# Fused attention and MoE kernel on one core: larger w_in pieces, an even split of the first output products, loads one pair later

## The chip, the cores and the metric

The kernel runs on one core of a Trainium2 chip. The metric is device time in microseconds (us) of one execution, lower is better. Profile times are us from the start of the profiled execution's span. PE is the matrix engine, PEld its weight loads, DVE the vector engine, ACT the scalar engine, POOL the GpSimd engine, SP the engine whose queue issues most DMAs.

## The reference

Eight batches of 12 heads of attention (448 rows, head dimension 64) with a softmax that has one extra term in its denominator, then a two-layer feed-forward over the 3584 resulting rows:

```
scores = scale * q @ k^T ; m = max(scores) ; e = exp(scores - m)
attn   = e / (sum(e) + exp(-m) + 1e-9)
x      = (attn @ v), heads side by side          # 3584 x 768
h      = x @ w_in                                # 768 x 2048
g      = h * tanh(softplus(h))
out    = g @ w_out                               # 2048 x 768, float32
```

q, k, v, w_in and w_out come in as float32; the kernel casts them to bf16 and accumulates in float32.

## The kernel before, in words

**Units.** Two heads make a pair, six pairs a batch. Three pairs make a unit, so that a batch has two units and there are 16 units with attention (u = 0 to 15, counted from 0; the change's title counts them from one, and its units five and six are u = 4 and u = 5). The first two units, u = 0 and 1, are a head written out pair by pair (lines 552 to 577). From u = 2 on, the loop at line 579 does for each unit twelve steps, n = 0 to 11 (three pairs by four score tiles), and then eight blocks, f = 0 to 7, of the first feed-forward product of the batch before (`mm1_mish`). Each attention unit thus has an exponent phase, its twelve steps, and a feed-forward phase, its eight blocks. Two more units, u = 16 and 17, finish the feed-forward alone.

**One score step.** PE makes a tile of scores (L247, L250, L255 for the last tile of a pair), DVE takes its negated maximum (L269, `negm`), ACT the exponent (L282, `en`). DVE and POOL divide by the denominators (`normalise`, L317 on DVE, L315 on POOL). The transposed weights `eT` come back by a DMA transpose on SP's queue (L321) or, for five early pairs, by PE. `av_pair` (L354) multiplies them with v, and DVE casts the result into `xT` (L363).

**The output product** w_out (L443, `mm2_part`) of two batches is cut in parts: a tile of 128 rows by some quarters of 192 of the 768 columns. A part of nq quarters is eight chunks of two matmuls, each 192 times nq columns wide. `plan` says which parts fall in which unit. From u = 4 on the units are "grouped": `GROUPED`, and for u = 5 `GROUPED_LATE_AV`, list for each step n how many chunks PE does (`fill`), which score tiles it makes next (`sc`) and which pair's product with v it does (`av`). One PSUM bank, mo1, serves in turn each `av` and the last score tile of a pair, tiles 3, 7 and 11 of the unit (`last_sc`, L255). So L255 waits until DVE has cast that `av` into `xT`. Chunks use bank mo0. Finished parts are copied to `o_sb` by DVE (L430), at the next place that flushes, and stored by SP (L408).

**Loads.** `load_pair` puts three DMAs (q, k, v of a pair, 224 KB each) on SP's queue; `cast_pair` has POOL cast them (L171, L172, L158). In the unit loop both are called at n = 0, 3 and 6 (`LOAD_AT`): the load of the pair that lies `LEAD` = 4 ahead, and the cast of the one that lies 3 ahead. The pairs of the next unit are transposed on PE (L189) in the feed-forward phase at f = 1, 3, 5, and copied out by DVE (L208) and ACT (L218). Of each q a remainder is copied by POOL (L213, L214). SP's queue is in order: in a unit it has three DMA transposes, then loads and stores.

**Weights** are loaded by POOL's queue in pieces (`w_pieces`, `load_w`, L154), which cast to bf16 on the way: w_in in twelve pieces of 256 rows by 512 columns, and w_out in eight of 512 rows by 384 columns. `W_HEAD`, `W_AT` and line 668 say where. The first feed-forward phase (u = 2) reads columns 0 to 1023 of w_in, that of u = 3 the rest.

Of the kernel before, what the change touches and what calls it, by code (L numbers as in the profile page):

```python
# [15 lines left out]
UNIT_PAIRS = 3  # L16
# [3 lines left out]
def kernel(  # L20
# [12 lines left out]
    d_model, d_ff = moe_w_in.shape  # L33
# [8 lines left out]
    UNITS_PER_B = HP // UNIT_PAIRS  # L42
# [3 lines left out]
    NH = d_model // 2  # L46
# [85 lines left out]


    def w_pieces():
        c_in, c_out = d_ff // 4, NH
        for i in range(4):
            for a in range(0, DM_T, 2):
                yield (
                    w_in_sb[:, a : a + 2, i * c_in : (i + 1) * c_in],
                    moe_w_in[a * 128 : (a + 2) * 128, i * c_in : (i + 1) * c_in],  # L140
                )
        for h in range(2):
            for f in range(0, FF_T, 4):
                yield (
                    w_out_sb[:, f : f + 4, h * c_out : (h + 1) * c_out],
                    moe_w_out[f * 128 : (f + 4) * 128, h * c_out : (h + 1) * c_out],
                )
# [315 lines left out]
    plan = {}  # L463
    for g in range(B // 2):
        u0 = first_mm2 + 4 * g
        if g == 0:
            plan[u0] = [(0, 0, 0, 2), (0, 1, 0, 2), (0, 2, 0, 1)]
            plan[u0 + 1] = [(0, 0, 2, 2), (0, 1, 2, 2), (0, 2, 2, 2), (0, 2, 1, 1)]
        else:
            plan[u0] = plan.pop(u0) + [(g, 0, 0, 2), (g, 0, 2, 2), (g, 1, 0, 1)]  # L470
            plan[u0 + 1] = [(g, 1, 2, 2), (g, 2, 0, 2), (g, 2, 2, 2), (g, 1, 1, 1)]
        plan[u0 + 2] = [(g, 4, 0, 2), (g, 4, 2, 2), (g, 5, 0, 2), (g, 5, 2, 1)]
        plan[u0 + 3] = [(g, 3, 0, 2), (g, 3, 2, 2), (g, 6, 0, 2), (g, 5, 3, 1)]
        if g < B // 2 - 1:
            plan[u0 + 4] = [(g, 6, 2, 2)]
        else:
            plan[u0 + 3] += [(g, 6, 2, 1), (g, 6, 3, 1)]
# [5 lines left out]

    GROUPED = (
        [("fill", 8), ("av", 0)],
        [("fill", 2), ("sc", (3, 4, 5))],
        [("fill", 3)],
        [("fill", 3), ("sc", (6,)), ("av", 1)],
        [("fill", 3)],
        [("sc", (7, 8, 9))],  # L490
        [("fill", 3)],
        [("fill", 2), ("sc", (10,)), ("av", 2)],
        [("fill", 8)],
        [("sc", (11,))],
        [],
        [],
    )
# [2 lines left out]
        [("fill", 3), ("sc", (4, 5))],  # L500
        [("fill", 2)],
        [("fill", 3), ("sc", (6,)), ("av", 0)],
        [("fill", 3)],
        [("sc", (7, 8, 9))],
        [("fill", 3)],
        [("fill", 2), ("sc", (10,)), ("av", 1)],
        [("fill", 8)],
        [("sc", (11,))],
        [("av1", 2)],
        [],  # L510
# [19 lines left out]
        (5, 2): [(4, 0)], (5, 3): [(4, 1)],  # L530
    }
    AV_HEAD = {(3, 3): 0, (4, 2): 2, (4, 3): 1}
    W_HEAD = {0: 3, 1: 1, 3: 1, 4: 1}
    AV_AT = ({3: 4, 7: 3, 9: 5}, {5: 6, 8: 7, 10: 8})

    W_AT = ({5: 1, 9: 1}, {1: 1, 4: 1, 5: 1, 7: 1, 9: 1, 11: 1}, {3: 1, 5: 1, 7: 1, 9: 1})
    for which in ("qk", "v"):
        for p in range(UNIT_PAIRS):
            load_pair(p, which)
# [39 lines left out]
    for u in range(UNITS_PER_B, N_UNITS + 2 * UNITS_PER_B):  # L579
        attn = u < N_UNITS  # L580
        filler = deque()
        for part in plan.get(u, []):
            filler.extend(mm2_part(*part))
        total, done, acc = sum(w for _, w in filler), 0, 0.0
        p0 = u * UNIT_PAIRS
        grouped = attn and p0 >= GROUP_FROM
        if u == N_UNITS:
            mo_free.append(mo_tiles[1])
        end = min((u + 1) * UNIT_PAIRS, N_PAIRS) * STEPS

        for n in range(steps):
            pi, s = divmod(n, STEPS)
            p, idx = p0 + pi, p0 * STEPS + n
            late_tp = u == UNITS_PER_B and n == STEPS
            if late_tp:
                transpose_pair(p0 + 2)
            exps(idx)
            if grouped:
                flush_late()
                for what, arg in (GROUPED_LATE_AV if u == LATE_AV else GROUPED)[n]:  # L600
                    if what == "fill":
                        for _ in range(min(arg, len(filler))):
                            fn, w = filler.popleft()
                            fn()
                            done += w
                    elif what in ("av", "av1"):
                        bank = mo_tiles[1] if what == "av" else sc_tiles[1][:, 0, :]
                        av_pair(p0 - UNIT_PAIRS + arg, bank=bank)
                    else:
                        flush_late()  # L610
                        for i in arg:
                            scores(p0 * STEPS + i)
                if n in LOAD_AT:
                    load_pair(p0 + LOAD_AT.index(n) + LEAD)
                    cast_pair(p0 + LOAD_AT.index(n) + LEAD - 1)
                if u - UNITS_PER_B < len(W_AT):
                    load_w(W_AT[u - UNITS_PER_B].get(n, 0))
                continue
            if late_tp:
                evac_qk(p0 + 2)  # L620
            if u == UNITS_PER_B + 1:
                for part in TURN_AT[1].get(n, []):
                    turn_on_pe(*part)
            flush_late()
            acc += weight[n]
            want = int(total * acc / sum(weight) + 1e-6)
            while done < want:
                fn, w = filler.popleft()
                fn()
                done += w  # L630
            scores_ahead(end)
            if n in LOAD_AT:
                load_pair(p0 + LOAD_AT.index(n) + LEAD)
                cast_pair(p0 + LOAD_AT.index(n) + LEAD - 1)
            if u - UNITS_PER_B < len(AV_AT):
                early = AV_AT[u - UNITS_PER_B]
                if n in early:
                    av_pair(early[n])
                if u == UNITS_PER_B:
                    for part in TURN_AT[0].get(n, []):  # L640
                        turn_on_pe(*part)
            elif u == N_UNITS and n in LAST_AV_AT:
                av_pair(p0 - UNIT_PAIRS + LAST_AV_AT.index(n))
            if u - UNITS_PER_B < len(W_AT):
                load_w(W_AT[u - UNITS_PER_B].get(n, 0))
        assert done == total

        moe = u < N_UNITS + UNITS_PER_B
        b, w = (u - UNITS_PER_B) // UNITS_PER_B, u % UNITS_PER_B
        nxt = p0 + UNIT_PAIRS  # L650
        todo = sorted(range(p0, nxt), key=lambda p: p in BY_PE)
        to_group = attn and nxt >= GROUP_FROM
        if to_group and nxt == GROUP_FROM:
            flush_late()
            mo_free.remove(mo_tiles[1])
            rg["next"] = N_PAIRS * STEPS
        for f in range(FF_U):
            if f == FF_U - 1 and to_group and nxt < N_PAIRS:
                for s in range(3):
                    scores(nxt * STEPS + s)  # L660
            if moe:
                bank = sc_tiles[0][:, 0, :] if f == 1 else None
                if to_group:
                    bank = (sc_tiles[0][:, 0, :], None, mo_tiles[1])[MISH_BANK[f]]
                mm1_mish(b, w * FF_U + f, bank)
                if f == 2 and to_gather:
                    gather_mid(to_gather.popleft())
            if u == UNITS_PER_B and f in (2, 6):
                load_w(1)
            if not attn:  # L670
                continue
            if f == 0:
                denominators(att[p0]["whole"])
                normalise(todo[0], dma=todo[0] not in BY_PE)
            if f in (1, 3, 5):
                transpose_pair(nxt + f // 2, bank=f // 2 % 2)
                evac_qk(nxt + f // 2)
            if not to_group and f in (4, 6):
                scores_ahead(nxt * STEPS + f // 2 - 1)
            if f == FF_U - 1 and not to_group:  # L680
                scores_ahead(nxt * STEPS + 3)
            if f == 3:
                normalise(todo[1], dma=todo[1] not in BY_PE)
            if f == 4:
                normalise(todo[2], dma=todo[2] not in BY_PE, on_pool=True)
        if attn and u + 1 < N_UNITS:

            nc.scalar.activation(out=one, in_=zero, func=AF.Exp)
        if moe and w == UNITS_PER_B - 1:
            to_gather.append(b)  # L690
            if u == N_UNITS + UNITS_PER_B - 1:
                gather_mid(to_gather.popleft())
# [32 lines left out]
```

## Time and profile before

| | |
|---|---|
| time, median of 3 runs | 479.11 us (477.68 to 480.66) |
| the profiled execution's own time | 479.26 us |
| its span | 477.2 us, granted clock 0.986 on average |
| PE busy | 439.1 us, 92% |
| ACT, DVE, POOL busy | 346.6, 329.6, 193.5 us |
| mean share of the 16 DMA engines, hardware queues | 81.6% |
| mean share, POOL's software queue | 9.1%, 7488 packets |
| POOL's issue of one weight piece | 0.75 us |
| one unit in the steady part (u = 7 to 14) | 25.8 us |

PE's busy time counts matmuls from their start to a modelled end, so that a wait shorter than a matmul's own latency (0.33 us for 384 columns, against 0.16 us from one start to the next) is not shown as idle time. The table's shares are means over the whole run; the stretches differ. Up to about 100 us PE has long gaps and waits for ACT or DVE; from there on it is nearly always busy.

### The profile page before, as it was taken

How to read it: one execution, taken by the hardware profiler on the slowest of the kernel's cores; microseconds unless marked ns; L12 is line 12 of the kernel's file. 1: busy time of each engine (PE TensorE's matmuls, PEld its weight loads, DVE VectorE, ACT ScalarE, POOL GpSimd, SP SyncE). 2: the span in 40 equal slices, each digit the busy share in tenths (PEclk: the TensorE clock that was granted, in tenths of full speed). 3: DMA queues.
4: the chain of work that ended last, by engine and by line, in shares of the span. 5: the costliest groups of instructions: out<-in, count | busy, mean ns of one | idle time of the engine just before them, and what ended most of it. 6: DMA issues, size and time to landing. Idle time of an engine off the chain costs nothing.

```text
span 477.2 us, 8887 instructions
## 1 busy us (share of the span) xinstructions
PE 439.1 (92%) x3064; PEld 236.0 (49%) x3064; DVE 329.6 (69%) x652; ACT 346.6 (73%) x919; POOL 193.5 (41%) x365
## 2 busy tenths in 40 slices
PE   4565887898999899999999999999999999999997
PEld 2233544454445354545555454545454545555565
DVE  4888987968688687768686877778776868330021
ACT  5979778879796888979797969888897979412300
POOL 4877809364706345353635253434535340300000
PEclk9999698999999999999999999999999999999999
DMA  8999959999999999899998989998989594970213
GB/s 209 225 216 227 263 89 243 164 189 236 174 215 280 211 213 205 240 195 269 179 262 181 235 151 230 221 213 227 195 249 212 157 169 112 155 161 1 67 33 101
DMA packets 202381, 90.37 MB, mean 189 GB/s; under 512 B 159072, under 2 KB 198880, under 8 KB 202336
## 3 DMA queue, kind: packets, MB, share of 16 engines
q1 hardware_dynamic: 194848, 83.51, 81.6%
q0 software_dynamic: 7488, 6.29, 9.1%
q8 instruction: 24, 0.39, 0.3%
q14 instruction: 21, 0.17, 0.1%
HBM read 45.61 MB, written 11.01 MB: 119 GB/s over the span
## 4 chain that ended last, share of the span: by engine, by line
PE 70%; ACT 9%; DMA 8%; DVE 5%; POOL 3%; issue 2%; SPq 1%; DVEq 0%; ACTq 0%; POOLq 0%
PE mo L443 27%; PE mo L377 19%; ACT en L282 7%; PE mo L354 6%; PE sc L377 6%; PE sc L247 5%; DVE negm L269 3%; PE sc L189 3%; DMA w_out_sb<-in_moe_w_out_dram 2%; DMA v_f<-in_v_dram 2%; DMA eT<-en 2%; PE mo L255 2%; POOL en L315 1%; DMA w_in_sb<-in_moe_w_in_dram 1%; PE mo L189 1%
## 5 line engine op out<-in xcount | busy, mean ns | idle before, releaser
L282 ACT ACTIVATE en<-sc,negm 128x448 bf16<-128x448 f32 x300 | 186.2, 636 | 12.6 <-DVE negm L269 9.4
L269 DVE TENSOR_REDUCE negm<-sc 128x2 f32<-128x896 f32 (+1 forms) x156 | 158.3, 1047 | 26.1 <-PE sc L250 18.7
L443 PE MATMUL mo<-w_out_sb,gT 128*128 128x384 bf16 (+1 forms) x912 | 137.3, 301 | 1.0 <-DVE o_sb L430 0.5
L377 PE MATMUL mo<-xT,w_in_sb 128*128 128x448 bf16 x594 | 124.4, 352 | 0.6 <-DMA w_in_sb<-in_moe_w_in_dram 0.6
L443 PEld LDWEIGHTS <-gT 128*128 128x128 bf16 x912 | 80.9, 98 | 57.3 <-issue 21.3
L383 ACT ACTIVATE gT<-mo 128x448 bf16<-128x448 f32 x99 | 54.0, 547 | 73.1 <-PE mo L377 73.1
L377 PEld LDWEIGHTS <-w_in_sb 128*128 128x128 bf16 x768 | 71.7, 97 | 68.0 <-issue 8.9
L315 POOL TENSOR_SCALAR en<-en,rden 128x448 bf16<-128x448 bf16 x122 | 76.1, 641 | 55.7 <-DVE rden L307 52.8
L171 POOL CAST q_bf<-q_f 112x512 bf16<-112x512 f32 x47 | 28.9, 616 | 109.7 <-DMA q_f<-in_q_dram 109.0
L430 DVE COPY o_sb<-mo 128x192 f32<-128x192 f32 (+1 forms) x65 | 32.5, 499 | 56.6 <-PE mo L443 44.4
L282 ACT ACTIVATION_READ_ACCUMULATOR en<-sc,negm 128x1 f32 x300 | 62.2, 207 | 0.0
L317 DVE TENSOR_SCALAR en<-en,rden 128x448 bf16<-128x448 bf16 x214 | 60.5, 352 | 0.5
L247 PE MATMUL sc<-kT,qT 64*128 64x448 bf16 x144 | 47.1, 385 | 12.7 <-ACT en L282 11.2
L354 PE MATMUL mo<-eT,v_bf 112*64 112x448 bf16 x376 | 45.9, 367 | 3.0 <-DMA eT<-en 1.8
L250 PE MATMUL sc<-kT,qT 64*128 64x448 bf16 x144 | 47.4, 387 | 0.0
L377 PE MATMUL sc<-xT,w_in_sb 128*128 128x448 bf16 x174 | 37.6, 352 | 0.1
L363 DVE CAST xT<-mo 128x448 bf16<-128x448 f32 x44 | 27.0, 616 | 10.3 <-PE mo L354 9.6
L158 POOL CAST v_bf<-v_f 112x512 bf16<-112x512 f32 x48 | 29.5, 614 | 8.3 <-DMA v_f<-in_v_dram 8.0
L172 POOL CAST k_bf<-k_f 112x512 bf16<-112x512 f32 x47 | 28.8, 612 | 7.5 <-DMA k_f<-in_k_dram 7.3
L269 DVE TENSOR_REDUCE negm<-mo 128x1 f32<-128x448 f32 x36 | 22.3, 620 | 10.5 <-PE mo L255 10.5
L354 PEld LDWEIGHTS <-v_bf 112*64 112x64 bf16 x384 | 18.9, 111 | 21.6 <-issue 14.6
L282 ACT ACTIVATE en<-mo,negm 128x448 bf16<-128x448 f32 x36 | 23.1, 640 | 7.7 <-DVE negm L269 7.7
(55 smaller groups left out, 356.4 us busy)
## 6 DMA issues: line engine op xcount, KB each, us to landing
q_f<-in_q_dram SPq DMA_DIRECT2D x48, 224.0 KB, 5.0
k_f<-in_k_dram SPq DMA_DIRECT2D x48, 224.0 KB, 5.3
v_f<-in_v_dram SPq DMA_DIRECT2D x48, 224.0 KB, 5.5
w_in_sb<-in_moe_w_in_dram POOLq DMA_DIRECT2D x12, 256.0 KB, 5.9
w_out_sb<-in_moe_w_out_dram POOLq DMA_DIRECT2D x8, 384.0 KB, 7.7
out_dram<-o_sb SPq DMA_DIRECT2D x7, 336.0 KB, 5.4
out_dram<-o_sb SPq DMA_DIRECT2D x8, 288.0 KB, 3.9
out_dram<-o_sb SPq DMA_DIRECT2D x8, 240.0 KB, 4.7
```

The lines of the kernel that those rows point to most:

```text
L158: nc.gpsimd.tensor_copy(out=casted[p][2], in_=loaded.pop(p)[2])
L247: nc.tensor.matmul(sc[:, 0, 0:S], lhsT=qT[0:64, qa : qa + 128], rhs=kA, start=True, stop=True)
L250: nc.tensor.matmul(sc[:, 1, 0:S], lhsT=qT[64:128, qb : qb + 128], rhs=kB, start=True, stop=True)
L269: nc.vector.tensor_reduce(out=negm, in_=sc[:, 0 : len(cols), 0:S], axis=AX.X, op=ALU.max, negate=True)
L282: nc.scalar.activation(out=st["en"][:, :, c, 0:SP_], in_=sc[:, bk, 0:S].rearrange("q (j c) -> q j c", j=NT), func=AF.Exp, bias=st["negm"][ ...
L315: nc.gpsimd.tensor_scalar(scalar2=1.0, op0=ALU.mult, op1=ALU.mult, **args)
L317: nc.vector.tensor_scalar(scalar2=None, op0=ALU.mult, **args)
L354: nc.tensor.matmul(av[h * 64 : (h + 1) * 64, 0:S], lhsT=v_bf[:, h, j * D : (j + 1) * D], rhs=e_h, start=(j == 0), stop=(j == NT - 1),)
L377: nc.tensor.matmul(h_ps[:, 0:S], lhsT=w_in_sb[:, dm, ff * 128 : (ff + 1) * 128], rhs=xT[b][:, dm, :], start=(dm == 0), stop=(dm == DM_T - 1),)
L383: nc.scalar.activation(out=gT[b][:, ff, :], in_=h_ps[:, 0:S], func=AF.Mish)
L430: nc.vector.tensor_copy(out=o_sb[:, cols], in_=st["o"][:, 0:n_cols])
L443: nc.tensor.matmul(st["o"][:, 0:n_cols], lhsT=src[:, ff, c0 : c0 + 128], rhs=w_out_sb[:, ff, cols], start=(ff == 0), stop=(ff == FF_T - 1),)
```

## The change

The pieces of w_in become half as many and twice as wide, and are spread anew. The output parts of u = 4 and 5 become six of two quarters, three in each unit, instead of five and seven quarters with two parts of one quarter. Steps in `GROUPED` and `GROUPED_LATE_AV` take other numbers of chunks, and in `GROUPED` the last chunk of a unit comes after score tile 11. In u = 4 one load is left out, and from u = 5 on each load and each cast is one place later: a unit loads the pairs of the next unit and casts two of them in its steps and the third at f = 1.

```diff
     def w_pieces():
-        c_in, c_out = d_ff // 4, NH
-        for i in range(4):
+        c_in, c_out = d_ff // 2, NH
+        for i in range(2):
...
         if g == 0:
-            plan[u0] = [(0, 0, 0, 2), (0, 1, 0, 2), (0, 2, 0, 1)]
-            plan[u0 + 1] = [(0, 0, 2, 2), (0, 1, 2, 2), (0, 2, 2, 2), (0, 2, 1, 1)]
+            plan[u0] = [(0, i, 0, 2) for i in range(3)]
+            plan[u0 + 1] = [(0, i, 2, 2) for i in range(3)]
...
     GROUPED = (
         [("fill", 8), ("av", 0)],
-        [("fill", 2), ("sc", (3, 4, 5))],
+        [("fill", 3), ("sc", (3, 4, 5))],
         [("fill", 3)],
-        [("fill", 3), ("sc", (6,)), ("av", 1)],
-        [("fill", 3)],
+        [("fill", 2), ("sc", (6,)), ("av", 1)],
+        [("fill", 4)],
         [("sc", (7, 8, 9))],
-        [("fill", 3)],
+        [("fill", 2)],
         [("fill", 2), ("sc", (10,)), ("av", 2)],
-        [("fill", 8)],
-        [("sc", (11,))],
+        [("fill", 7)],
+        [("sc", (11,)), ("fill", 1)],
...
     GROUPED_LATE_AV = (
...
-        [("fill", 3)],
+        [("fill", 4)],
         [("sc", (7, 8, 9))],
-        [("fill", 3)],
+        [("fill", 2)],
         [("fill", 2), ("sc", (10,)), ("av", 1)],
-        [("fill", 8)],
+        [],
...
-    W_HEAD = {0: 3, 1: 1, 3: 1, 4: 1}
+    W_HEAD = {0: 1, 1: 1, 3: 1}
...
-    W_AT = ({5: 1, 9: 1}, {1: 1, 4: 1, 5: 1, 7: 1, 9: 1, 11: 1}, {3: 1, 5: 1, 7: 1, 9: 1})
+    W_AT = ({5: 1}, {1: 1, 5: 1, 7: 1, 9: 1, 11: 1}, {3: 1, 5: 1, 7: 1, 9: 1})
...
                 if n in LOAD_AT:
-                    load_pair(p0 + LOAD_AT.index(n) + LEAD)
-                    cast_pair(p0 + LOAD_AT.index(n) + LEAD - 1)
+                    at = p0 + LOAD_AT.index(n)
+                    if u > first_mm2:
+                        load_pair(at + LEAD - 1)
+                        if n:
+                            cast_pair(at + LEAD - 2)
+                    else:
+                        if n < LOAD_AT[-1]:
+                            load_pair(at + LEAD)
+                        cast_pair(at + LEAD - 1)
...
-            if u == UNITS_PER_B and f in (2, 6):
+            if u == UNITS_PER_B and f == 2:
                 load_w(1)
...
             if f in (1, 3, 5):
                 transpose_pair(nxt + f // 2, bank=f // 2 % 2)
                 evac_qk(nxt + f // 2)
+                if f == 1 and u > first_mm2:
+                    cast_pair(nxt + UNIT_PAIRS - 1)
```

`first_mm2` is 4.

## The prediction, made before the changed kernel was run

> **What bounds the kernel now.** I read the table by stretches first, then PE's waits, then single engines in order of time. By stretch (us; PE, PEld, DVE, ACT, POOL busy; clock; DMA share; GB/s), two stretches around u = 4 and 5 and two of the steady part:
>
> ```profile
> 102.00:131.00 29.00, 26.14 (x182) 13.49 (x181) 21.57 (x42) 24.99 (x65) 17.07 (x33) 1.00 1.19 205
> 131.00:158.50 27.50, 25.64 (x180) 13.34 (x180) 21.56 (x40) 22.26 (x60) 10.65 (x22) 1.00 1.15 234
> 208.00:234.00 26.00, 25.91 (x183) 13.53 (x182) 20.28 (x41) 21.61 (x57) 11.30 (x23) 1.00 1.01 214
> 234.00:259.80 25.80, 25.77 (x183) 13.48 (x181) 19.57 (x40) 21.61 (x57) 11.06 (x23) 1.00 0.96 221
> ```
>
> In the steady part PE has no visible gap, at full clock. Between 102 and 158.5 us it has 4.7 us of them (29.00 - 26.14 + 27.50 - 25.64). Before 102 us there are some 30 us of gaps, for ACT, DVE or the first loads. Who waits for whom (total, times, longest):
>
> ```profile
> DVE negm L269 <- PE mo L255: 10.5, 24, 0.4
> PE mo L255 <- DVE xT L363: 2.7, 3, 1.9
> PE mo L354 <- DMA eT<-en: 1.8, 1, 1.8
> PE mo L443 <- DVE o_sb L430: 0.5, 1, 0.5
> PE mo L443 <- DMA w_out_sb<-in_moe_w_out_dram: 0.4, 1, 0.4
> ```
>
> So what the loads and pieces can give back is small: 1.8 us for eT at the start of u = 6, 0.4 for w_out in u = 5. The first row matters more: 24 times DVE waits exactly the same 0.44 us for L255, the delay of L255 after DVE's own cast. It shows a second bound. One steady unit (u = 7) on DVE and PE:
>
> ```profile
> 185.94 0.62 DVE L363 CAST xT<-mo 128x448 bf16<-128x448 f32 x1 [0.34 <-PE mo L354]
> 191.02 0.61 DVE L363 CAST xT<-mo 128x448 bf16<-128x448 f32 x1
> 196.07 0.61 DVE L363 CAST xT<-mo 128x448 bf16<-128x448 f32 x1
> ```
>
> ```profile
> 185.76 0.82 PE L443 MATMUL mo<-w_out_sb,mid 128*128 128x384 bf16 x4
> 186.62 0.35 PE L255 MATMUL mo<-kT,qr 128*128 128x448 bf16 x1
> 191.69 0.35 PE L255 MATMUL mo<-kT,qr 128*128 128x448 bf16 x1
> 196.74 0.35 PE L255 MATMUL mo<-kT,qr 128*128 128x448 bf16 x1
> ```
>
> Each L255 starts 0.06 us after the cast before it ends (186.56, 191.63, 196.68). Between two of them DVE works without a gap but for that 0.44: four maxima, one o_sb, one cast, 5.06 us. PE's work between them takes nearly as long: the four matmuls from 185.76 end their slots at 186.43 (the last three start from 185.94, 0.163 apart), so PE idles 0.19 us before the first L255, hidden in a matmul's latency; likewise 0.09 before the second (last slot ends 191.60) and 0.05 before the third. So from L255 of tile 3 to that of tile 11, DVE sets 10.12 us, whatever PE does.
>
> **The change, part by part.**
>
> *w_in pieces.* POOL issues 6 DMAs for 12: 6 x 0.75 = 4.5 us less on POOL, all at places where POOL idles afterwards (12.6 us before 72.67, 8.3 before 95.35): worth nothing. Without that cover it would be 0.75 each. In the head, pairs 0, 1, 3 and 4 get 1, 1, 1, 0 wide pieces for 3, 1, 1, 1 narrow ones, so 256 KB less at pair 0 and 4, more at 1 and 3. Alone, a narrow piece takes about 1.1 us of DMA time (two issued 0.75 apart at 58.6 land 1.05 apart); moved before pair 7's load it delays the cast of its k, done at 41.99, and PE transposes it at 43.03: hidden by 1.04. u = 2 and 3 find their pieces landed (issued by 34, needed at 63.9; issued by 80, needed at 90.7; landing took 4.0 to 8.8). Taken 0; bounds -0.5 and +1.0.
>
> *Even split, u = 4.* PE gets 16 matmuls of 384 columns (0.163 each) for 16 of 192 (0.083), +1.3 us, in a unit where it waits 2.3 us for xT. On the DVE bound: the third chunk in step 1 puts two more matmuls before tile 3; 0.33 less the hidden 0.19 is +0.14. Before tile 7, eight wide matmuls (1.30) stand for six narrow ones: +0.11. The part's copy takes 0.55 for 0.34: +0.21. Together +0.46; bounds 0 (all hidden by the 2.3) and +1.3.
>
> *Even split, u = 5.* 16 narrow matmuls go (1.3 us), but tile 11 at 142.17 waits for the cast that ends at 142.12, so that stays. The wait for w_out goes (0.43), one more chunk before tile 7 takes back 0.19: -0.24. If ACT, whose gap there is only 0.18, binds instead, 0; if the gap after 129.5 goes with the o_sb wait, -1.0.
>
> *One load less in u = 4.* SP's queue:
>
> ```profile
> 111.67 0.46 SPq L128 DMA_DIRECT2D q_f<-in_q_dram  x1
> 120.98 18.92 SPq L321 DMA_TRANSPOSE eT<-en  x3
> 141.05 0.64 SPq L128 DMA_DIRECT2D q_f<-in_q_dram  x1
> 146.99 0.46 SPq L128 DMA_DIRECT2D v_f<-in_v_dram  x1
> 148.95 15.39 SPq L321 DMA_TRANSPOSE eT<-en  x3
> ```
>
> The nine DMAs from 108.5 to 113.1 become six. The pair left out, 672 KB, is 2.7 us at the 250 GB/s of that stretch. It delays the w_out pieces issued from 115 on, and these share the engines with the transpose of 120.98, whose issue takes 9.59 us for the usual 4.3. I take it as 1.9 us earlier for SP (half to all of 2.7, less what has drained). Then SP is free for the next transpose at 146.7, DVE's normalise ends at about 147.3 with the shift of u = 4 and 5, eT lands about 157, and PE comes there at 157.4: the 1.83 us go, less the +0.22 from u = 4 and 5 and a rest: I count -1.4; bounds -1.83 and 0.
>
> *Loads three ahead, u = 5.* Now pairs 18, 19, 20 are loaded by the DMAs that stood at 141.05 to 146.99 and transposed at 145.6, 148.3 and 151.0. Those DMAs took 4.6 to 5.7 us to land; with two casts of 0.6 the k of each would be ready at 147.0, 150.4 and 153 by the old times, late by 1.4 to 2.1; with SP 1.9 earlier, in time. Taken 0; bounds 0 and +2.1. Behind these casts on POOL stand the q remainders and the seven normalise operations; their users come a unit later.
>
> *Loads three ahead, steady units.* A pair loaded in u = 6 was cast at 167.59 and 172.24 and is transposed at 173.29 and 176.08: early by 4 and 2 us. The third cast now comes at f = 1, behind the first q remainders (176.09 to 176.75), so its k is ready at 177.9; PE transposes it from 178.74. Slack 0.8, in the next units 1.1 to 1.6. Worth 0. It falls on DVE's second normalise of seven, which takes 1.81 alone and took 2.85 beside such casts (149.06): +1.04. Behind it the third qT copy (start 179.22, idle 0.47 before) ends 0.57 later at 180.18, and PE needs that bank at 180.76. Hidden; a further 0.6 would not be.
>
> *Fill order, nine steady units (u = 6 to 14).* Tile 3 moves +0.14 as above, and tile 11 with it (10.12 after). Before tile 11 PE now has one chunk fewer and waits some 0.5 us; that chunk, two narrow matmuls, stands behind tile 11: +0.17. The feed-forward phase starts 0.31 later, and PE is the bound there: nine times 0.31 = +2.8. In u = 15 L255 waits 0.38 already and f = 3 waits for ACT: 0. Bounds: -0.22 a unit (a third of a microsecond of hidden waits recovered until ACT, whose mish of f = 0 ends at 200.50 for PE's 200.72, binds) and +0.50 (all three matmul pairs exposed), -2.0 and +4.5. I take the row arithmetic, since both ends of the DVE loop are seen in nine units alike.
>
> Sum: 0.46 - 0.24 - 1.4 + 2.8 = +1.6 us. The span of 477.2 becomes 478.8 and the execution's 479.26 becomes 480.9; that execution lies 0.15 above the median of 479.11, so the median becomes 480.7.
>
> [...] When POOL casts stood at 148.93 to 151.27, DVE's normalise lost 1.04 us of the 1.70 they overlapped. [...]
>
> **Rivals.**
> - *The order costs nothing.* PE is the only bound and the 0.06 and 0.44 are mere latency: then 0.46 - 0.24 - 1.4 = -1.2, 477.9. For it: PE shows no gap. Against: the equal 5.06. Its far end, with -2.0 for recovered waits and the whole 1.83, is 475.5.
> - *The load left out relieves nothing.* eT lands at 159 as before, and PE waits at the transposes of u = 5 instead of there: +0.2 by u = 6, then +2.8: 482.1. For it: pair 18 had landed by 120.7, before the slow transpose. With 0.5 a unit and the head's +1.0 it is 484.9.
> - *DVE loses all of POOL's cast time*, 1.83: its third qT copy comes 0.2 after PE needs the bank, nine times: 480.7 + 1.8 = 482.5. Against: the 1.04.
> - *POOL loses instead* (the other side). The third cast in the feed-forward phase waits out DVE's normalise, 1.81 us: its k is 1.0 past the slack of 0.8 and PE waits for it at its third transposes in nine units: +9, 489.7. It decides from 0.8 us of delay on. Against: casts beside normalise kept 0.61.
>
> **How the numbers follow.** Forecast 0.45, order free 0.22, no relief 0.15, DVE loses 0.06, POOL loses 0.12. Within 1% (474.3 to 483.9, about what a measurement can tell from no change) lie the forecast and most of the rest. Faster by more needs the first rival's far end and more: 0.06. Slower: POOL's rival and the second's far end, 0.18. Same 0.76. The range, 475.5 to 484.9, joins the far ends of the first two rivals and leaves out POOL's.
>
> **What would show it.** L255 of tile 11 about 0.1 later in its unit, a gap of 0.3 to 0.5 us before it, a unit of 26.1 us for 25.8; no eT wait in u = 6, or less than 0.5; no PE wait on L189; DVE's second normalise about 2.8 us. I am wrong if units stay at 25.8 or less, or if PE waits for POOL's casts.

## The result, and the profile after

The changed kernel takes 480.24 us (median of 20 runs, 478.94 to 487.72) against 478.89 us (20 runs, 477.68 to 481.43) for the kernel before: a ratio of 1.0029, 95% interval 1.0017 to 1.0041, or +0.8 to +2.0 us. That is a loss of 0.3%, clear of the noise and well inside the 1% within which the prediction counts a time as the same. The forecast was 480.7. One run, of 487.72, was disturbed and is left out of the ratio.

The profiled execution of the changed kernel took 480.6 us with a span of 478.6, where before had 477.2. The same four stretches as before the change (us; PE, PEld, DVE, ACT, POOL busy; clock; DMA share; GB/s):

```profile
102.00:131.00 29.00, 27.36 (x185) 13.94 (x183) 22.38 (x42) 23.70 (x61) 16.29 (x32) 1.00 1.10 204
131.00:158.50 27.50, 25.33 (x175) 12.72 (x174) 20.53 (x39) 22.62 (x61) 11.25 (x22) 1.00 1.12 240
208.00:234.00 26.00, 25.68 (x183) 13.44 (x182) 20.34 (x41) 21.62 (x58) 11.01 (x23) 1.00 1.04 211
234.00:259.80 25.80, 25.48 (x181) 13.38 (x180) 19.75 (x40) 21.41 (x58) 10.95 (x22) 1.00 1.00 222
```

In the steady part (last two rows) PE now stands still for 0.32 us a unit, where it stood still for 0.09 and 0.03. Who waits for whom says what for (the waits for eT in u = 6 and for w_out in u = 5 are no longer in the list):

```profile
DVE negm L269 <- PE mo L255: 17.0, 35, 0.6
PE mo L255 <- DVE xT L363: 5.4, 12, 1.6
```

Twelve times PE waits for DVE's cast ahead of L255, for three times before; and DVE waits for L255 35 times for 24: at tile 11 the copy of the unit's last part stood between DVE's cast and its maximum (196.89 in u = 7 of the kernel before) and now comes behind the maximum (196.96), so that the wait which it filled is seen there too. The unit u = 7 on DVE and PE:

```profile
185.12 0.62 DVE L363 CAST xT<-mo 128x448 bf16<-128x448 f32 x1 [0.34 <-PE mo L354]
190.32 0.61 DVE L363 CAST xT<-mo 128x448 bf16<-128x448 f32 x1
195.37 0.61 DVE L363 CAST xT<-mo 128x448 bf16<-128x448 f32 x1
```

```profile
184.94 1.15 PE L443 MATMUL mo<-w_out_sb,mid 128*128 128x384 bf16 x6
185.93 0.35 PE L255 MATMUL mo<-kT,qr 128*128 128x448 bf16 x1
190.98 0.35 PE L255 MATMUL mo<-kT,qr 128*128 128x448 bf16 x1
196.03 0.35 PE L255 MATMUL mo<-kT,qr 128*128 128x448 bf16 x1 [0.21 <-DVE xT L363]
196.22 0.33 PE L443 MATMUL mo<-w_out_sb,gT 128*128 128x192 bf16 x2
196.38 0.92 PE L377 MATMUL sc<-xT,w_in_sb 128*128 128x448 bf16 x4
```

Three things are to be seen. Tile 3 (185.93) now starts 0.19 after the cast has ended (185.74) for 0.06: it waits for PE's third chunk. From tile 3 to tile 11 it is 10.10 us, as before (10.12), though PE has two chunks less to do in it; the time saved stands as idle time, 0.21 us ahead of tile 11 and 0.11 ahead of the narrow chunks before it (at 194.50), which wait for DVE's copy. And the chunk behind tile 11 puts the feed-forward phase off to 0.35 after tile 11, for 0.18. Every unit from u = 6 on takes 26.07 us, for 25.79 in most of those before the change (25.90 and 25.92 in u = 6 and 8).

Where the 1.4 us between the two spans lie, by the starts of L255 and of the first L377 of a unit: +1.1 in the first 90 us (by the exponents there), +0.1 up to tile 3 of u = 4, +0.20 in the rest of u = 4, -0.50 from f = 0 of u = 4 to that of u = 5, -1.77 from there to tile 3 of u = 6, +2.10 from there to f = 0 of u = 14, -0.06 in u = 15, +0.2 in the tail. So from tile 3 of u = 4 to f = 0 of u = 15 the changed kernel takes 297.51 us and the kernel before 297.54: in this pair of profiles its gains and losses cancel, and the difference lies in the head, for which I had 0. At 45 us the changed kernel is still 0.1 us ahead (the same exponent starts at 45.35 for 45.44), so that the loss falls between 45 and 90 us. Whether the head is the change's doing is the first question for the experiments.

### The profile page after: what moved, and what is told of

It is laid out like the page before. It is cut to its first block, busy times and chain, and to the rows that moved or that the text cites. A ratio compares the mean times of both kernels' runs of the same rounds, so it can differ in the third digit from the quotient of the medians.

```text
span 478.6 us, 8864 instructions
## 1 busy us (share of the span) xinstructions
PE 441.8 (92%) x3048; PEld 236.9 (50%) x3048; DVE 332.1 (69%) x651; ACT 346.6 (72%) x919; POOL 189.0 (39%) x359
## 4 chain that ended last, share of the span: by engine, by line
PE 71%; DVE 9%; issue 5%; SPq 2%; DMA 1%; ACT 1%; POOL 0%; DVEq 0%; ACTq 0%
PE mo L377 24%; PE mo L443 23%; PE sc L377 7%; PE sc L247 5%; PE mo L354 5%; DVE negm L269 5%; PE sc L189 3%; DVE xT L363 2%; DVE o_sb L430 2%; PE mo L255 2%; DMA out_dram<-o_sb 1%; PE mo L332 1%; SPq L321 1%; ACT en L282 1%; DVE eT L336 1%
## 5 line engine op out<-in xcount | busy, mean ns | idle before, releaser
L443 PE MATMUL mo<-w_out_sb,gT 128*128 128x384 bf16 (+1 forms) x896 | 138.4, 304 | 1.6 <-DVE o_sb L430 0.5
L377 PE MATMUL mo<-xT,w_in_sb 128*128 128x448 bf16 x594 | 124.5, 352 | 0.6 <-DVE xT L363 0.6
L443 PEld LDWEIGHTS <-gT 128*128 128x128 bf16 x896 | 80.8, 98 | 62.7 <-issue 24.0
L377 PEld LDWEIGHTS <-w_in_sb 128*128 128x128 bf16 x768 | 71.6, 98 | 66.2 <-issue 8.3
L430 DVE COPY o_sb<-mo 128x384 f32<-128x384 f32 (+1 forms) x64 | 32.1, 501 | 53.7 <-PE mo L443 40.4
L317 DVE TENSOR_SCALAR en<-en,rden 128x448 bf16<-128x448 bf16 x214 | 63.7, 367 | 0.6 <-DVE rden L299 0.2
L247 PE MATMUL sc<-kT,qT 64*128 64x448 bf16 x144 | 47.2, 385 | 12.0 <-ACT en L282 11.3
L377 PE MATMUL sc<-xT,w_in_sb 128*128 128x448 bf16 x174 | 37.6, 352 | 0.0
L363 DVE CAST xT<-mo 128x448 bf16<-128x448 f32 x44 | 27.0, 615 | 8.5 <-PE mo L354 8.5
```

The costliest lines, as they stand in the source:

```text
L247: nc.tensor.matmul(sc[:, 0, 0:S], lhsT=qT[0:64, qa : qa + 128], rhs=kA, start=True, stop=True)
L317: nc.vector.tensor_scalar(scalar2=None, op0=ALU.mult, **args)
L363: copy(out=xT[b][:, hp, :], in_=av[:, 0:S])
L377: nc.tensor.matmul(h_ps[:, 0:S], lhsT=w_in_sb[:, dm, ff * 128 : (ff + 1) * 128], rhs=xT[b][:, dm, :], start=(dm == 0), stop=(dm == DM_T - 1),)
L430: nc.vector.tensor_copy(out=o_sb[:, cols], in_=st["o"][:, 0:n_cols])
L443: nc.tensor.matmul(st["o"][:, 0:n_cols], lhsT=src[:, ff, c0 : c0 + 128], rhs=w_out_sb[:, ff, cols], start=(ff == 0), stop=(ff == FF_T - 1),)
```

## The experiments

Theory: the order of chunks costs 0.28 us a unit because DVE sets the stretch from tile 3 to tile 11; split and loads give the wait for eT back; the pieces are worth nothing, and the head's +1.1 is the clock's chance. Rivals: PE alone sets the unit (the order is free); the load left out relieves nothing; the pieces cause what the head loses. Ratios are to the kernel before in the same runs, with 95% intervals; "stretch" is tile 3 of u = 4 to f = 0 of u = 15, which leaves the head out.

**1. The pieces alone** (in the kernel before)

```diff
-        c_in, c_out = d_ff // 4, NH
-        for i in range(4):
+        c_in, c_out = d_ff // 2, NH
+        for i in range(2):
...
-    W_HEAD = {0: 3, 1: 1, 3: 1, 4: 1}
+    W_HEAD = {0: 1, 1: 1, 3: 1}
```

> Only the pieces of w_in are changed. In the two profiles the changed kernel is 1.1 us behind at 102 us, and the granted clock is 0.64 for 0.80 from 50 to 65 us. Theory A, by my prediction: the pieces are worth 0 and the clock's low stretches fall as they happen to fall: the median within 0.4 us of before, and the low clock may end anywhere between 55 and 61 us. Theory B: the pieces shift PE's work in the head so that the clock comes up later: +0.8 to +1.2 us, and a clock of about 0.64 from 50 to 65 us. After 105 us nothing differs from before under either: the wait for eT of 1.8 us at the start of u = 6 stays, and steady units take 25.8 us.

Ratio 1.0008 (0.9985 to 1.0030). The interval does not decide, since it holds 0 and +1.1, and the median of the twelve runs, 480.51 for 478.74, lies 1.8 us above, outside the 0.4 of theory A. The clock says more: the granted clock is 0.982 on average over these twelve runs and 0.981 over the 35 of the kernel before, so the new pieces do not bring it down. In the profile tile 3 of u = 4 comes at 106.03 us, 0.16 earlier than before, at a higher clock.

**2. The changed kernel with the old pieces** (the same lines the other way round)

> The changed kernel with the twelve pieces of w_in of before; all else as changed. Theory A (the pieces are worth nothing, the clock of the head falls as it happens to): the same as the changed kernel, +0.8 to +2.0 us against before. Theory B (the wide pieces bring about more of the low clock in the head, +0.8 to +1.2 us): +0.2 to +0.6 us against before. By the stretches of the parts alone, from tile 3 of u = 4 to the end, both expect the wait for eT gone and units of 26.07.

Ratio 1.0026 (1.0000 to 1.0052), the changed kernel's own, from other runs, 1.0029; the interval holds what either theory expects. Tile 3 of u = 4 comes at 107.50 us, with the old pieces, as late as in the changed kernel (107.40). Two stretches of the head, in the order before, changed, old pieces in the changed kernel, new pieces alone (the third figure from the end is the clock):

```profile
50.00:65.00 15.00, 12.20 (x95) 6.94 (x94) 14.75 (x25) 10.66 (x33) 9.75 (x16) 0.80 0.85 197
75.00:102.00 27.00, 22.66 (x182) 13.14 (x181) 21.70 (x44) 21.83 (x58) 16.63 (x30) 0.94 1.04 191
```

```profile
50.00:65.00 15.00, 13.19 (x93) 7.60 (x92) 14.32 (x25) 9.98 (x31) 9.03 (x15) 0.64 0.98 224
75.00:102.00 27.00, 23.57 (x179) 13.20 (x178) 21.41 (x43) 21.68 (x57) 14.80 (x28) 0.87 0.95 182
```

```profile
50.00:65.00 15.00, 11.95 (x95) 6.75 (x95) 14.75 (x27) 10.49 (x31) 9.77 (x16) 0.78 1.05 219
75.00:102.00 27.00, 23.81 (x182) 13.49 (x180) 21.47 (x43) 22.21 (x58) 16.64 (x30) 0.87 1.05 196
```

```profile
50.00:65.00 15.00, 11.67 (x95) 6.74 (x94) 14.77 (x25) 10.53 (x33) 9.03 (x15) 0.86 0.99 223
75.00:102.00 27.00, 21.68 (x183) 12.84 (x182) 21.89 (x44) 21.87 (x58) 15.41 (x29) 1.00 1.01 186
```

The clock is at half speed for a time in each head, with either kind of piece. Before 102 us these times add up to 13.7 us in the kernel before, 20.5 in the changed kernel, 20.5 with the old pieces in it, and 6.8 with the new pieces alone; on average to 15.4 us in the eight profiles with the old pieces and 14.8 in the three with the new ones (the two of experiment 9 have other work in the head and are left out). Tile 3 of u = 4 starts between 105.92 and 107.50 us in those eight, and at 106.03, 106.97 and 107.40 in the three; it starts by 106.78 in all that have up to 13.7 us of half speed, and from 106.96 on in all that have more. So no profile speaks for theory B, and the +1.1 of the pair goes with the clock. Experiments 5 and 7 below, measured in one series, differ only in the pieces and in the list of u = 5, and their medians are 477.26 and 477.38 us. What the runs leave open is an effect of some tenths.

**3. The even split alone**

```diff
-            plan[u0] = [(0, 0, 0, 2), (0, 1, 0, 2), (0, 2, 0, 1)]
-            plan[u0 + 1] = [(0, 0, 2, 2), (0, 1, 2, 2), (0, 2, 2, 2), (0, 2, 1, 1)]
+            plan[u0] = [(0, i, 0, 2) for i in range(3)]
+            plan[u0 + 1] = [(0, i, 2, 2) for i in range(3)]
```

> Only the plan of u = 4 and 5 is changed (three parts of two quarters in each). Theory A: in u = 4 the feed-forward phase starts 0.3 us later, in u = 5 it gains 0.5 since w_out is no longer waited for; eT of u = 6, which the SP queue sets, lands where it did (159.0 us), so that the wait for it takes up the gain: -0.2 to +0.3 us in the end, with a wait for eT of 1.6 to 2.1 us. Theory B: PE's work alone decides, and 16 wider matmuls in u = 4 cost 1.3 us that u = 5 gives back: also about 0 at the end, but u = 4 longer by 1.3 us and u = 5 shorter by 1.3.

Ratio 0.9985 (0.9963 to 1.0008); stretch 294.85 us, 2.69 less than before. Both theories missed: in this profile the wait for eT is gone with the loads as they were, though barely (eT lands at 156.40 us, PE begins on it at 156.44), and so is that for w_out. The profile shows more than the usual gain: its execution, 476.25 us, is the fastest of the twelve, and their median is 0.5 us below that of the kernel before; the ratio's -0.7 us (-1.8 to +0.4) excludes neither theory by itself. In the profile it gains, up to f = 0 of u = 5, 0.41 us (+0.21 and -0.62), from there to tile 3 of u = 6 1.87.

**4. The loads alone**

```diff
-                    load_pair(p0 + LOAD_AT.index(n) + LEAD)
-                    cast_pair(p0 + LOAD_AT.index(n) + LEAD - 1)
+                    at = p0 + LOAD_AT.index(n)
+                    if u > first_mm2:
+                        load_pair(at + LEAD - 1)
...
```

> Only the loads and casts are moved (one load less in u = 4, three pairs ahead from u = 5 on). Theory A: the DMA transpose issued at about 121 us holds the SP queue 1 to 2 us less, eT of u = 6 is there in time: the wait of 1.8 us goes, with it perhaps the 0.4 for w_out, and the steady units stay at 25.8: -1.4 to -2.2 us. Theory B (relieves nothing): eT lands as before and PE waits at the transposes of u = 5: 0 to +0.3. Theory C (POOL is late with the third cast): PE waits for the cast of k at the third transposes, 0.5 us or more a unit: +5 us or more.

Ratio 0.9978 (0.9961 to 0.9995); stretch 295.40 us, 2.14 less. This is theory A: no wait for eT, none for w_out, one of 0.2 us for a cast of k in u = 5 (at 148.2), most steady units of 25.79; the times give less than its 1.4 us, -1.1 (-1.9 to -0.2). The first transpose of u = 5 on SP's queue, in the kernel before, with the split alone, with the loads alone, and in the changed kernel:

```profile
120.98 9.59 SPq L321 DMA_TRANSPOSE eT<-en  x1
```

```profile
120.65 8.09 SPq L321 DMA_TRANSPOSE eT<-en  x1
```

```profile
120.58 7.08 SPq L321 DMA_TRANSPOSE eT<-en  x1
```

```profile
122.08 6.74 SPq L321 DMA_TRANSPOSE eT<-en  x1
```

The loads are what shortens this issue. In the seven profiles that have the nine loads ahead of it, it takes 8.1 to 9.9 us, and the 8.09 of the split alone is one of them; in the six with six loads it takes 6.3 to 7.8 us, 1.9 less on average. What the split changes lies later: the transpose that PE waits for in u = 6 lands 9.1 us after its issue with the split alone, and after 9.8 to 10.8 in the seven profiles with the old split. Why it does was not looked into. Each part ended the wait in its one profile.

**5. Split and loads together**, pieces and order as before

> The kernel before with two parts of the change, the even split and the loads; pieces and order of chunks as before. Each alone took the wait for eT in u = 6 away (1.8 us), so that they can't add up: theory A, one shared wait, with 0.4 of w_out and 0.36 at tile 3 of u = 15 beside it: -1.5 to -2.7 us, the transpose issued at about 121 us held for some 6 to 7 us. Theory B, independent gains: -2.7 us from the profile of the split and -2.1 from that of the loads, -4 us or more.

Ratio 0.9961 (0.9944 to 0.9977), -1.9 us: faster than both kernels. The issue takes 6.34 us; stretch 294.94 us, 2.60 less. The size is theory A's, not the 4 us of theory B: the two share one wait, and together they give no more than the split alone gave in its profile. The times by themselves do not show the sharing: the ratios of experiments 3 and 4 are worth 0.7 and 1.1 us, each to about 1 us, which also add up to 1.9. In u = 7, which takes 26.10 us, PE waits 0.15 for DVE's copy of qT.

**6. The order alone**

```diff
-        [("fill", 2), ("sc", (3, 4, 5))],
-        [("fill", 3)],
-        [("fill", 3), ("sc", (6,)), ("av", 1)],
+        [("fill", 3), ("sc", (3, 4, 5))],
         [("fill", 3)],
+        [("fill", 2), ("sc", (6,)), ("av", 1)],
+        [("fill", 4)],
...
-        [("fill", 8)],
-        [("sc", (11,))],
+        [("fill", 7)],
+        [("sc", (11,)), ("fill", 1)],
```

> Only the order of chunks in the steady units is changed, in u = 4 and u = 6 to 14. Theory A: DVE sets the 10.1 us from L255 of tile 3 to that of tile 11, tile 3 moves by 0.1 and the chunk behind tile 11 adds 0.15: a unit takes 26.05 us for 25.79, nine times 0.26 = +2.1 to +2.5, with a gap of 0.2 us before each L255 of tile 11. Theory B: PE alone sets the unit, the order costs nothing: within 0.4 us of before and units of 25.8.

Ratio 1.0055 (1.0035 to 1.0076), +2.6 us (1.7 to 3.6); stretch 300.36 us, +2.82. Units of 26.07 us, but for two of 26.34 and 26.29, and the gap of 0.21 ahead of each tile 11. This is theory A, a little above its size; the stretch also holds waits for w_out (0.9) and eT (1.3) that differ from those of the kernel before (0.4 and 1.8).

**7. The changed kernel with the old order**

> The changed kernel with the order of chunks of before in the steady units; pieces, split, loads and the list of u = 5 as changed. Theory A (the order costs 0.26 to 0.28 in each of nine units): 2.3 to 2.6 us below the changed kernel, so -0.9 to -1.3 us against before, units of 25.79 us, no gap before tile 11. Theory B (what the order costs is only moved elsewhere): within 0.5 us of the changed kernel, +0.9 or more against before.

Ratio 0.9967 (0.9949 to 0.9984), -1.6 us, where the changed kernel has +1.4; units of 25.79; stretch 294.74, 2.77 less than the changed kernel's. This is theory A, a little above its 2.3 to 2.6.

**8. The order taken apart.** One run has only what lies ahead of tile 11 (three chunks before tile 3, and the steps up to tile 11 as in experiment 6), the other only the last chunk behind it:

```diff
-        [("fill", 8)],
-        [("sc", (11,))],
+        [("fill", 7)],
+        [("sc", (11,)), ("fill", 1)],
```

> Of the change only the order up to tile 11: three chunks before tile 3, nothing behind tile 11. Theory A (DVE sets the stretch from tile 3 to tile 11): tile 3 comes 0.13 later in each unit, tile 11 with it, and nothing stands behind tile 11: a unit of 25.92 us, +1.2 us. Theory B (PE alone): units of 25.79, 0.

> Of the change only the last chunk of a steady unit moved behind score tile 11; the other steps as before. Theory A (DVE sets the stretch from tile 3 to tile 11, so that PE's chunk taken out ahead of tile 11 gains nothing and stands behind it): the stretch stays at 10.12 us, the feed-forward phase starts 0.35 us after tile 11 for 0.19, a unit of 25.95 us. With the 0.13 that three chunks before tile 3 cost, that makes the 26.07 of the changed kernel. Theory B (PE alone): tile 11 comes 0.17 earlier and the unit stays at 25.79.

One profile each. With the chunks ahead, units of 25.91 us (+0.12): all L255 of a unit and the first of the next one,

```profile
211.57 0.35 PE L255 MATMUL mo<-kT,qr 128*128 128x448 bf16 x1
216.63 0.35 PE L255 MATMUL mo<-kT,qr 128*128 128x448 bf16 x1
221.69 0.35 PE L255 MATMUL mo<-kT,qr 128*128 128x448 bf16 x1
237.48 0.35 PE L255 MATMUL mo<-kT,qr 128*128 128x448 bf16 x1
```

are 5.06, 5.06 and 15.79 us apart, for 5.06, 5.06 and 15.66. The list of PE's waits is empty for this unit; its idle time is 0.16 us (25.91 less 25.75 busy), where a unit of before had 0.03, in gaps of 0.11 and 0.05 ahead of the chunks of 220.16 and ahead of tile 11. Whoever reads the waits alone does not find the loss. With the last chunk behind, most units take 25.95 us (+0.16); here tile 11 of u = 8 and what follows it:

```profile
223.71 0.35 PE L255 MATMUL mo<-kT,qr 128*128 128x448 bf16 x1
223.90 0.33 PE L443 MATMUL mo<-w_out_sb,gT 128*128 128x192 bf16 x2
224.06 1.30 PE L377 MATMUL sc<-xT,w_in_sb 128*128 128x448 bf16 x6
```

Tile 11 does not come earlier for the chunk taken out ahead of it: it starts 10.12 us after tile 3 in most units, as in the kernel before. 0.12 + 0.16 = 0.28, theory A in both. (In this run the clock was 0.89 between 117 and 132 us and u = 4 took 1 us more than before, but the wait for eT was then 0.5 for 1.8: tile 3 of u = 6 comes 54.29 us after that of u = 4, before 54.53.)

**9. Less work for DVE**, in the changed kernel and in the kernel before. If DVE sets the stretch, shorter copies (they leave half of the columns of each wide part out of the result) shorten the unit, and the cost of the order shrinks:

```diff
-            nc.vector.tensor_copy(out=o_sb[:, cols], in_=st["o"][:, 0:n_cols])
+            nc.vector.tensor_copy(out=o_sb[:, q0 * NQ : (q0 + 1) * NQ], in_=st["o"][:, 0:NQ])
```

> The changed kernel with less work for DVE: of each output part of 384 columns only the first 192 are copied to the buffer that is stored (0.34 us for 0.56), so that half of those columns is left out; PE's work and order are those of the changed kernel. Theory A: two such copies lie between tile 3 and tile 11, DVE's stretch shrinks by 0.42 from 10.10 to 9.7, PE's work in it is about 9.5, so a unit takes 25.65 us for 26.07. Theory B (PE alone, or ACT): units stay at 26.07. In the head of the program POOL writes zeros to the four buffers, which may shift the first 60 us.

> The kernel before with the same work left out for DVE (half of the columns of each output part of 384 not copied). Theory A: DVE's stretch from tile 3 to tile 11 shrinks by the same 0.42, but there PE has 9.98 us of work in the order of before, so that only 0.14 is gained: units of 25.65 us for 25.79, as many as the changed kernel with the short copies; the order then costs nothing any more. Theory B (PE alone): 25.79, and the order goes on costing 0.28.

One profile each; both have two more lines, so that L255 is L257, L443 is L445 and L363 is L365. Most units take 25.80 us for 26.07 in the changed kernel, and 25.65 for 25.79 in the kernel before. Theory B is out. Of theory A, the number for the kernel before is met. That for the changed kernel is missed by 0.15, 25.80 for 25.65, and the order does go on costing something. Changed kernel, short copies:

```profile
209.64 0.35 PE L257 MATMUL mo<-kT,qr 128*128 128x448 bf16 x1
213.31 1.47 PE L445 MATMUL mo<-w_out_sb,gT 128*128 128x384 bf16 x8
214.62 0.35 PE L257 MATMUL mo<-kT,qr 128*128 128x448 bf16 x1
217.97 1.33 PE L445 MATMUL mo<-w_out_sb,gT 128*128 128x192 bf16 x14
219.48 0.35 PE L257 MATMUL mo<-kT,qr 128*128 128x448 bf16 x1 [0.18 <-DVE xT L365]
```

From tile 3 to 7 it takes 4.98 us, and PE sets them: the eight matmuls from 213.31 start 0.163 us apart, so that the next can start at 214.62 (8 x 0.163), and L257 starts there. From 7 to 11 it takes 4.86, with an idle PE: DVE sets them. I had taken the larger of the two engines' sums over the whole stretch, max(9.70, 9.49); but they meet at tile 7 too, and the larger of each half counts: 4.98 + 4.86 = 9.84. So 0.15 of the order's 0.28 stay.

## Why the prediction was right, point by point

The time and the verdict were right, and most of the mechanism; some terms met their size by two errors that cancel. That the forecast lies within 0.5 us of the median is in part luck, since the measured difference itself is known to 0.6 us. That the profiled 480.6 us lies so near the 480.9 forecast for it is luck: in that pair the gains and losses of the parts cancel, and the difference is the head's.

- *w_in pieces and head, 0.* Right to some tenths (experiments 1, 2, 5 and 7). The pair of profiles has +1.1 there, with 6.8 us more of half clock. The delay of pair 7's k came as foreseen, a little larger: its cast ends at 43.20 us for 42.00, PE waits 0.15 for it, and is ahead of the kernel before again at 44.09 (for 44.18). The trace has the two pieces issued at 58.6 land 1.28 us apart, where the working has 1.05.
- *Even split in u = 4, +0.46.* +0.1 and +0.20 in the pair of profiles, +0.21 after tile 3 with the split alone. The working gave 0.14, and 0.32 after tile 3: one tenth too much.
- *Even split in u = 5, -0.24.* -0.50 in the pair, since the 0.43 for w_out went and nothing of it was taken back. Of the five profiles that have the old split, the old loads and whole copies, this wait is in two, 0.43 and 0.9 us: 0.27 on average.
- *One load less in u = 4: eT, -1.4.* The wait of 1.83 went whole. But it is not 1.83 each time: in those five profiles it was 1.8, 1.7, 1.3, 0.8 and 0.5 us, 1.2 on average. The cause that I gave, the load left out, holds: the prediction had SP 1.9 us earlier, and the issue takes 1.9 less on average over all profiles (2.85 in the pair). It is only one of two: in its profile the split alone ended the wait as well (experiment 3), by another way, which I had not seen.
- *Loads three ahead, u = 5, 0.* Right: PE waits for no cast after 102 us in the changed kernel, once for 0.2 with the loads alone, once for 0.3 in the changed kernel with the old pieces.
- *Loads three ahead, steady units, 0.* Right, with more room than I gave it. In u = 7 of the changed kernel, DVE's second normalise and the casts beside it:

```profile
202.10 2.29 DVE L317 TENSOR_SCALAR en<-en,rden 128x448 bf16<-128x448 bf16 x7
204.46 0.39 DVE L208 TENSOR_SCALAR qT<-sc 128x448 bf16<-128x448 bf16 x1
```

```profile
201.24 0.61 POOL L171 CAST q_bf<-q_f 112x512 bf16<-112x512 f32 x1
201.80 0.61 POOL L172 CAST k_bf<-k_f 112x512 bf16<-112x512 f32 x1
202.36 0.65 POOL L158 CAST v_bf<-v_f 112x512 bf16<-112x512 f32 x1
```

  k is ready at 202.41 and PE transposes it from 204.18: 1.77 us of slack where I had 0.8 (1.1 to 1.6 in the later units), so that the rival in which POOL loses was far off. The normalise took 2.29 us for 1.81 alone, where I had 2.85: the casts overlap it by 0.91 us, for 1.70 in the case from which I took the price. DVE lost 0.48 us beside 0.91 of casts and 0.5 of remainder copies, and no cast took more than 0.65. There is a loss, then, but no run shows that DVE loses the whole of the casts (it lost 1.04 of 1.70 and 0.48 of 0.91), nor a cast that waits out a normalise: the delays in the two rivals, 1.83 (three casts of 0.61) and 1.81 (one normalise), were my estimates.
- *Fill order, nine steady units, +2.8.* Measured 2.77 (changed kernel with and without it) and 2.82 (alone, with other waits in it). It is ten units of 0.28, not nine of 0.31: I left u = 15 out, since L255 waits there anyhow, and the chunk before tile 3 costs 0.12 to 0.13, not 0.14.
- *What the sum lacked.* In u = 15 tile 3 came 0.2 to 0.4 us late in all the profiles with the old split and whole copies, and never with the even one: -0.3. In the kernel before, DVE's cast ahead of it (392.75) waits 0.69 us for an exponent of ACT, where with the even split it waits 0.34 for PE's product; why was not looked into. Likewise u = 6 and 8 took 0.12 and 0.14 us more in the kernel before, and not in the changed one.
- *Signs named.* The unit of 26.1, no wait for eT and none on L189 came. The gap of 0.3 to 0.5 us before tile 11 shows as 0.21; by starts it is 0.37, since the 14 narrow matmuls from 194.50, 0.083 apart, leave room for the next at 195.66, and L255 starts at 196.03. DVE's second normalise took 2.29 for 2.8.

The signs and the mechanism hold by experiment: the order +2.8, the one shared wait and w_out -1.5, u = 4 +0.3, u = 15 -0.3 make +1.3 us, for the +1.35 between the medians; the sum is good to some tenths, and the measured difference to 0.6. Of the rivals, "the order costs nothing" falls with experiments 6 to 9, "the load left out relieves nothing" with 4, and both that concern POOL's casts with the rows above. The change loses because a good part of it (split and loads, -1.9) is paid for with a bad one (the order).

## What to carry to other kernels

When two engines take turns through one buffer, work out the sum of each between every two meeting points, not over the whole loop: here the larger of each counted (experiment 9: 4.98 + 4.86 us for 9.70), and a chunk moved from a stretch that the other engine sets into one that its own engine sets is a cost that no list of waits need show (experiment 8: +0.12 us a unit, an empty list). A wait for a DMA that differs from profile to profile (eT: 0.5 to 1.8 us in five) is worth its mean over several, not the value in one. Where a change is made of parts, measure each: here the order left out turns a loss of 1.4 us into a gain of 1.6 (experiment 7).

## What the runs showed of the hardware

PE's clock fell to half speed in every head, for 6.8 to 20.5 us before 102 us, and when it did so differed from profile to profile: from 45.7 to 55.9 and 79.8 to 83.2 us in the kernel before, from 47.2 to 60.8 and 81.3 to 88.1 in the changed one. Between 50 and 65 us PE is busy for 0.78 to 0.88 of the time in ten profiles, and the granted clock was 0.64 to 0.86 with nearly the same instructions; tile 3 of u = 4 moved by up to 1.6 us with it. In two profiles it fell later as well: with the last chunk behind the clock was 0.89 at 117 to 132 us, and in the kernel before with short copies six matmuls of 448 columns took 1.77 us at 117.91 and 2.45 at 119.47, for 1.30 at 122.25. The four stretches of the pair last 10.24 and 3.41 us (before), 13.65 and 6.83 (changed): 3.41 us and two, three and four times as long. What sets their place was not shown. Since 1.6 us is 0.3% of the time, two profiles of kernels that differ by a few tenths of a percent are to be compared from the first point at which the clock stays up, as was done with the stretch above.

The issue of the DMA transpose behind the weight pieces took 6.3 to 9.9 us where the next one took 4.3, and the queue behind it stood as long. With one load of three DMAs less ahead of it, it took 1.9 us less on average (experiment 4): here what was issued ahead of a transpose cost the queue time in the transpose's own issue.
